# Two extra rows of the last weight matrix for half the partitions, and less work on VectorE, in a one-core decode layer

## The chip, the cores and the metric

The kernel runs on one core of a Trainium2 chip. The metric is the device time of one execution in microseconds, as the median of several runs. One further execution is profiled: its trace holds every instruction of the five engines (PE, the matrix engine; DVE, the vector engine; ACT, the scalar engine; POOL, GpSimd; SP, the queue engine that issues most transfers), every packet of the DMA engines, and every semaphore update. "The span" is the time from the first to the last recorded instruction of that execution.

## What is computed

One decode step of a transformer layer with four sequences and one token each: layer normalisation, attention of 32 query heads over the last 2048 rows of a cache with 4 key-value heads, a residual, a second layer normalisation, and a gated feed-forward block.

```python
D, Hq, Hkv, Sk, Dh, F = 1024, 32, 4, 8192, 128, 3584      # B = 4, Sq = 1, all bfloat16
W = 2048
q = (layernorm(x) @ wq).reshape(B, Sq, Hq, Dh).transpose(0, 2, 1, 3)
k = jnp.repeat(k_cache[:, :, Sk - W:, :], Hq // Hkv, axis=1)
v = jnp.repeat(v_cache[:, :, Sk - W:, :], Hq // Hkv, axis=1)
p = softmax(einsum("bhqd,bhkd->bhqk", q, k) * Dh ** -0.5)
h = x + einsum("bhqk,bhkd->bhqd", p, v).transpose(0, 2, 1, 3).reshape(B, Sq, Hq * Dh) @ wo
n = layernorm(h)
out = h + (silu(n @ w1) * (n @ w3)) @ w2
```

With four tokens there is little arithmetic for each weight. What has to be read is some 55.6 MB: 8 MB each of k, v, wq and wo (in units of 1,048,576 bytes, as below), and 7 MB each of w1, w3 and w2.

## The kernel before

**The ring of slots.** All large inputs pass through five slots of SBUF of 128 partitions x 32 KB (4 MB each). `ring` (line 107) lists what goes into them in order: k in two slots, half of wq, two slots for the transposed keys (no transfer), the other half of wq, v in two slots, wo in two, w1, w3 and w2 in two each. `fill` (line 119) issues the transfers on SP's queue, in the order of the list, as soon as all users of the slot five places earlier are done; `done` calls it after each user. Thus a transfer is issued when a slot comes free, and waits in the DMA queues behind those issued earlier.

**How w2 is cut.** w2 has 3584 rows of 1024 values (2 KB). Line 79 gives each of the 128 partitions 28 rows. They are loaded in pieces of 16, 8, 2 and 2 rows (`W2B`, line 108): the first piece fills one slot, the other three share the last one.

**Order of the work.** The schedule is written by hand: on every engine the instructions run in the order of the program.

- x is loaded by ACT's queue into `x_nat` (line 149), and the constants are made on DVE and GpSimd (lines 152 to 190).
- `layernorm_T` (line 192) is used twice. It works on transposed data; DVE makes nearly all steps.
- Lines 235 to 247: the keys are transposed by PE, block by block (8 matmuls each, 32 blocks), and copied out of PSUM by DVE and ACT in turn.
- Lines 250 to 282: the query projection, and the masked queries `Qm`.
- Lines 290 to 405: attention, one batch row after the other in a pipeline: `scores`, `row_max` (maximum, turned and shared out by two small matmuls), `softmax` (four exponentials on ACT, with their sums in `rs`), `transpose_p` on DVE, `output` (the sum's reciprocal, 16 matmuls over v, then `od` and `om` on DVE).
- Lines 406 to 444: the outputs are rearranged and multiplied by wo.
- Lines 450 to 482: the second layer normalisation, w1, the sigmoid (exponential, plus one, reciprocal, product), w3, the product `hg`, and its transposed form `hg_T`.
- Lines 485 to 504: the product with w2, piece by piece, the residual, and the store by two queues.

Each weight matmul handles a quarter of the output columns: four matmuls in four column groups of the array (`tile_position=(0, R * c)`) share one pass.

Of the kernel before, what the change touches and what calls it, by code (L numbers as in the profile page):

```python
# [10 lines left out]
P = 128  # L11
ACT = mybir.ActivationFunctionType
ALU = mybir.AluOpType
# [10 lines left out]
def kernel(  # L24
# [30 lines left out]
    FC = F // P  # L55
    NK = W // P
    C = 4
# [3 lines left out]
    FQ = F // C  # L61
    FH = FQ // 2
    assert B == C and Hkv == C and B * Hq == P and Dh == P and REP * Hkv == R
    assert D == KC * P and F == FC * P and W == NK * P and NQ == Hq * Dh
# [14 lines left out]
    w2_v = B_w2.rearrange("(p fc) n -> p fc n", fc=FC)  # L79
# [21 lines left out]
    wo_ = pair([("wo", g, [1, T * D], wo_v[:, g : g + 1, :]) for g in range(Hkv)])  # L101
# [6 lines left out]
    W2B = [16, 8, 2, 2]  # L108
# [5 lines left out]
    ring += [w2_[:1], w2_[1:]]  # L114
# [4 lines left out]
    def fill():  # L119

        while len(taken) < len(ring):
# [6 lines left out]
            for name, i, shape, src in parts:  # L128
# [3 lines left out]
                if src is not None:  # L132
                    nc.sync.dma_start(out=dst if name in ("k", "v") else view, in_=src)  # L133
# [6 lines left out]
    def done(name, i):  # L140
# [7 lines left out]
    nc.vector.memset(x_nat[:], 0.0)  # L148
    nc.scalar.dma_start(out=x_nat[::S, :], in_=x_flat.rearrange("b (c n) -> c b n", c=C))
    fill()  # L150

    ident = const.tile([P, P], BF16)
    make_identity(nc, ident[:])
    ones_f = const.tile([P, P], FP32)
    nc.vector.memset(ones_f[:], 1.0)
    eps_t = const.tile([P, 1], FP32)
    nc.vector.memset(eps_t[:], eps)

    t32 = const.tile([P, R], FP32)
    nc.vector.tensor_reduce(  # L160
        out=t32[:], in_=ident[:].rearrange("p (q h) -> p h q", q=C), axis=AX.X, op=ALU.add
    )
    ident_f = const.tile([P, P], FP32)
    nc.gpsimd.tensor_copy(out=ident_f[:], in_=ident[:])
    same = const.tile([P, C, R], FP32)
    for q in range(C):
        nc.gpsimd.tensor_copy(out=same[:, q], in_=t32[:])
# [4 lines left out]
    nc.vector.tensor_scalar(  # L172
# [3 lines left out]
    nc.vector.tensor_reduce(  # L176
        out=jmask[:, :, 0], in_=ident[:].rearrange("p (j h) -> p j h", j=JM), axis=AX.X, op=ALU.add
    )
    nscale = const.tile([P, Hkv], FP32)
    nc.vector.memset(nscale[:], -qscale)  # L180
# [3 lines left out]
    for l in range(2):  # L184
        nc.gpsimd.tensor_copy(
# [5 lines left out]

    def layernorm_T(h_T, tag):

        both = act.tile([P, 2, KC, B], FP32, tag=tag + "_both")
        nc.vector.tensor_copy(out=both[:, 0], in_=h_T[:, :, ::S])
        nc.vector.tensor_tensor(out=both[:, 1], in0=both[:, 0], in1=both[:, 0], op=ALU.mult)  # L196
        sums_ps = ps.tile([P, 2, KC, B], FP32, tag="kt3")
        nc.tensor.matmul(sums_ps[:], lhsT=ones_f[:], rhs=both[:], start=True, stop=True)  # L198
        sums = act.tile([P, 2, B], FP32, tag=tag + "_sums")
        nc.vector.tensor_reduce(  # L200
            out=sums[:], in_=sums_ps[:].rearrange("p t k b -> p t b k"), axis=AX.X, op=ALU.add
        )
        mean = act.tile([P, 2, B], FP32, tag=tag + "_mean")
        nc.vector.tensor_single_scalar(out=mean[:], in_=sums[:], scalar=1.0 / D, op=ALU.mult)
        rstd = act.tile([P, 1, B], FP32, tag=tag + "_rstd")
        nc.vector.tensor_tensor(out=rstd[:, 0], in0=mean[:, 0], in1=mean[:, 0], op=ALU.mult)
# [7 lines left out]
        hc = act.tile([P, KC, B], FP32, tag=tag + "_hc")  # L214
# [20 lines left out]
    for b in range(B):  # L235
        k = get("k", b)
        kT = get("kT", b)
        for jb in range(JR // JB):
# [3 lines left out]
            if n_step % 2 == 0:  # L242
                nc.vector.tensor_copy(out=kT[:, jb * JB : (jb + 1) * JB], in_=kt_ps[:])  # L243
            else:
                nc.scalar.copy(out=kT[:, jb * JB : (jb + 1) * JB], in_=kt_ps[:])  # L245
# [4 lines left out]
    q_ps = [ps.tile([P, REP // 2, Dh], FP32, tag=f"sc{hf}", name=f"q_ps{hf}") for hf in range(2)]  # L250
    HALF = REP // 2
    for i in range(KC // 4):
        w = get("wq", i)
        for kk in range(4):
            kc = 4 * i + kk
            for hf in range(2):
                for c in range(C):
                    o = (2 * c + hf) * HALF * Dh
                    nc.tensor.matmul(  # L259
                        q_ps[hf][R * c : R * c + R],  # L260
# [8 lines left out]
    nc.vector.tensor_copy(out=q_sb[:, :HALF], in_=q_ps[0][:])  # L269
    nc.scalar.copy(out=q_sb[:, HALF:], in_=q_ps[1][:])  # L270
# [7 lines left out]
    for b in range(B):  # L278
        nc.vector.tensor_copy(  # L279
            out=Qm[:, b].rearrange("p (g y) -> p g y", y=QW)[:, :, :REP],  # L280
# [254 lines left out]
```

## Time and profile before

| | |
|---|---|
| runs, median (3) | 139.9 us (139.68 to 140.05) |
| the profiled execution | 140.13 us |
| its span | 138.3 us |
| PE / DVE / ACT / POOL busy | 58% / 38% / 31% / 3% of the span |
| HBM read | 55.58 MB, 402 GB/s over the span |
| first data packet, last weight landing | 2.2 us, 134.26 us |

The costliest groups of instructions by busy time are ACT's exponentials (L334, 16 of them, 19.7 us), PE's matmuls over v (L369, 17.5 us), the key transposes (L241, 17.3 us), ACT's copies of the transposed keys (L245, 16 of 1.01 us) and DVE's (L243, 16 of 0.69 us). DVE's single longest instruction is the reciprocal of the sigmoid (L474, 5.75 us).

The profile page divides the span into 40 slices and gives for each engine the busy share in tenths; the DMA row is the mean over the core's 16 DMA engines. A line of a "windows" view has the stretch in microseconds, its length, the busy time (and number of instructions) of PE, PEld (weight loads), DVE, ACT and POOL, the granted clock of PE as a share of full speed, the DMA engines' mean share, and the rate. A line of the timeline has the start, the length, the engine, the line of the program, what was done, and in brackets the idle time before it and what ended it.

### The profile page before, as it was taken

The numbers are of one execution on the slowest core, as the hardware profiler recorded it, in microseconds if no ns is written. First come the engines' busy times: TensorE is split into PE (matmuls) and PEld (weight loads), VectorE is DVE, ScalarE is ACT, GpSimd is POOL, SyncE is SP. The second block draws the span as 40 slices with busy tenths as digits, with TensorE's granted clock in tenths as the row PEclk, the third lists the DMA queues.
The fourth block names the chain that finished last, engine by engine and source line by source line (L and its number), as shares of the span: only waits on it lengthen the run. The fifth ranks groups of instructions, "written<-read, shape, count | busy, mean of one in ns | idle before, by whom it ended". The sixth has DMA issues, their size and how long they took to land.

```text
span 138.3 us, 2012 instructions
## 1 busy us (share of the span) xinstructions
PE 80.2 (58%) x866; PEld 47.5 (34%) x868; DVE 52.9 (38%) x97; ACT 42.7 (31%) x57; POOL 4.2 (3%) x18
## 2 busy tenths in 40 slices
PE   0029898921903889328918998659539901703780
PEld 0029887820301322014304434537324400202550
DVE  3036676520000235177087197540330298350001
ACT  3005988850000325998807900000040200000000
POOL 7400000000000000000000000000000000000000
PEclk9999999998555799975797799965865896555555
DMA  4999999999989999999999999999999999999930
GB/s 152 399 423 431 431 436 455 455 441 398 445 384 426 441 417 417 450 407 431 450 400 431 433 469 431 394 448 448 419 398 448 456 411 430 445 407 398 406 148 2
DMA packets 3217, 55.72 MB, mean 403 GB/s; under 512 B 360, under 2 KB 392, under 8 KB 648
## 3 DMA queue, kind: packets, MB, share of 16 engines
q1 hardware_dynamic: 3178, 55.58, 94.4%
q8 instruction: 7, 0.11, 0.3%
q10 hardware_dynamic: 30, 0.01, 0.0%
q14 instruction: 2, 0.02, 0.0%
HBM read 55.58 MB, written 0.01 MB: 402 GB/s over the span
## 4 chain that ended last, share of the span: by engine, by line
DMA 49%; PE 27%; DVE 13%; ACT 4%; SPq 3%; issue 2%; DVEq 0%
DMA s_wq<-in_A_wq_dram 29%; DMA s_w<-in_B_w_dram 20%; PE o_ps L369 10%; PE y_ps L434 5%; ACT P L334 4%; PE sc_ps L294 3%; DVE PT L346 3%; SPq L133 3%; PE gu_ps L458 2%; PE q_ps L259 2%; DVE om L386 2%; DVE od L378 2%; PE on_ps L409 1%; PE tot_ps L355 1%; PE nm_ps L323 1%
## 5 line engine op out<-in xcount | busy, mean ns | idle before, releaser
L334 ACT ACTIVATE P<-sc_ps,bias 128x512 bf16<-128x512 f32 x16 | 19.7, 1417 | 9.6 <-DVE bias L331 9.6
L241 PE MATMUL kt_ps<-ident,s_k 128*128 128x128 bf16 x256 | 17.3, 228 | 1.3 <-ACT s_kT L245 1.0
L369 PE MATMUL o_ps<-s_v,PT 128*128 128x512 bf16 x62 | 17.5, 439 | 0.3 <-issue 0.2
L241 PEld LDWEIGHTS <-s_k 128*128 128x128 bf16 x256 | 16.3, 103 | 2.3 <-issue 1.7
L245 ACT COPY s_kT<-kt_ps 128x1024 bf16<-128x1024 bf16 x16 | 15.7, 1012 | 2.5 <-PE kt_ps L241 2.5
L458 PE MATMUL gu_ps<-s_w,n_T 128*32 128x448 bf16 x128 | 10.7, 513 | 8.8 <-DMA s_w<-in_B_w_dram 6.8
L259 PE MATMUL q_ps<-s_wq,n_T 128*32 128x512 bf16 x64 | 7.0, 615 | 11.8 <-DMA s_wq<-in_A_wq_dram 11.8
L243 DVE COPY s_kT<-kt_ps 128x1024 bf16<-128x1024 bf16 x16 | 11.1, 693 | 5.8 <-PE kt_ps L241 5.8
L491 PE MATMUL y_ps<-s_w,hg_T 128*32 128x256 bf16 x112 | 6.6, 418 | 8.0 <-DMA s_w<-in_B_w_dram 8.0
L369 PEld LDWEIGHTS <-PT 128*128 128x128 bf16 x64 | 7.2, 117 | 9.2 <-issue 4.4
L346 DVE STREAM_TRANSPOSE PT<-P 128x2048 bf16<-128x2048 bf16 x4 | 9.2, 2303 | 2.7 <-ACT P L334 2.7
L208 ACT ACTIVATE rstd<-rstd,eps_t 128x4 f32<-128x4 f32 x2 | 0.6, 297 | 29.5 <-DVE rstd L207 29.5
L458 PEld LDWEIGHTS <-n_T 128*32 128x32 bf16 x128 | 4.7, 131 | 14.1 <-issue 11.6
L294 PE MATMUL sc_ps<-s_kT,Qm 128*32 128x512 bf16 x64 | 8.5, 603 | 0.4 <-DVE Qm L279 0.4
L491 PEld LDWEIGHTS <-hg_T 128*32 128x32 bf16 x112 | 4.9, 142 | 10.0 <-issue 5.9
L259 PEld LDWEIGHTS <-n_T 128*32 128x32 bf16 x64 | 2.7, 137 | 15.6 <-issue 15.5
L269 DVE CAST q_sb<-q_ps 128x512 bf16<-128x512 f32 x1 | 0.7, 692 | 18.3 <-PE q_ps L259 18.3
L198 PE MATMUL sums_ps<-both,ones_f 128*128 128x64 f32 x4 | 1.1, 373 | 11.2 <-DVE both L196 11.2
L434 PE MATMUL y_ps<-s_wo,oP 128*32 128x256 bf16 x128 | 6.5, 397 | 1.7 <-DVE oP L422 1.7
L378 DVE SCALAR_TENSOR_TENSOR od<-o_ps,rinv,jmask 128x512 f32<-128x512 f32 x4 | 3.0, 751 | 8.4 <-PE o_ps L369 8.3
L270 ACT CAST q_sb<-q_ps 128x512 bf16<-128x512 f32 x1 | 0.6, 585 | 17.8 <-PE q_ps L259 17.8
L310 PE MATMUL mx_ps<-ident_f,rmax 128*1 128x128 f32 x8 | 1.7, 302 | 7.4 <-DVE rmax L308 7.4
(68 smaller groups left out, 64.7 us busy)
## 6 DMA issues: line engine op xcount, KB each, us to landing
s_w<-in_B_w_dram SPq DMA_DIRECT2D x4, 3584.0 KB, 21.2
s_k<-in_A_k_cache_dram SPq DMA_DIRECT2D x4, 2048.0 KB, 16.1
s_wq<-in_A_wq_dram SPq DMA_DIRECT2D x2, 4096.0 KB, 35.3
s_v<-in_A_v_cache_dram SPq DMA_DIRECT2D x4, 2048.0 KB, 25.1
s_wo<-in_A_wo_dram SPq DMA_DIRECT2D x4, 2048.0 KB, 25.5
s_w<-in_B_w_dram SPq DMA_DIRECT2D x1, 4096.0 KB, 28.0
s_w<-in_B_w_dram SPq DMA_DIRECT2D x1, 2048.0 KB, 25.7
s_w<-in_B_w_dram SPq DMA_DIRECT2D x2, 512.0 KB, 27.0
```

Of the source, the lines that this page charges most:

```text
L241: nc.tensor.transpose(out=kt_ps[:, jj], in_=k[:, jb * JB + jj, :], identity=ident[:])
L243: nc.vector.tensor_copy(out=kT[:, jb * JB : (jb + 1) * JB], in_=kt_ps[:])
L245: nc.scalar.copy(out=kT[:, jb * JB : (jb + 1) * JB], in_=kt_ps[:])
L259: nc.tensor.matmul(q_ps[hf][R * c : R * c + R], lhsT=xn_T[:, kc, :], rhs=w[:, kk, o : o + HALF * Dh], start=(kc == 0), stop=(kc == KC - 1) ...
L294: nc.tensor.matmul(sc_ps[b][R * q : R * q + R], lhsT=Qm[:, b, g * R : (g + 1) * R], rhs=v[:, g, q], start=(g == 0), stop=(g == Hkv - 1), t ...
L334: nc.scalar.activation(out=P4[:, :, :, g], in_=sc_ps[b][:].rearrange("p (j i) -> p j i", i=L5), func=ACT.Exp, bias=bias[:, g : g + 1], sca ...
L346: nc.vector.transpose(out=PT[:].rearrange("p j h -> p (j h)"), in_=stage.pop(("P4", b))[:].rearrange("p j i g -> p (j i g)"),)
L369: nc.tensor.matmul(o_ps[:], lhsT=PT[:, i * JM : (i + 1) * JM, :].rearrange("p j h -> p (j h)"), rhs=v[:, i * JM : (i + 1) * JM, :], start= ...
L378: nc.vector.scalar_tensor_tensor(out=od[:], in0=o_ps[:], scalar=rinv[:, 0:1], in1=jmask[:].to_broadcast([P, JM, Dh]), op0=ALU.mult, op1=AL ...
L434: nc.tensor.matmul(y_ps[R * c : R * c + R, :], lhsT=oP[:, g, t, :], rhs=w[:, 0, o : o + DQ], start=(g == 0 and t == 0), stop=(g == Hkv - 1 ...
L458: nc.tensor.matmul(out_ps[hf][R * c : R * c + R], lhsT=hn_T[:, kc, :], rhs=w[:, kk, o : o + FH], start=(kc == 0), stop=(kc == KC - 1), til ...
L491: nc.tensor.matmul(y2_ps[R * c : R * c + R, :], lhsT=hg_T[:, fc, :], rhs=w[:, ff, c * DQ : (c + 1) * DQ], start=(fc == 0), stop=(fc == FC ...
```

## The change

It has several parts.

1. **w2.** The 128-row grid loses a row: each partition holds 27 rows (pieces of 16, 7, 2 and 2), and the 128 rows that remain go to partitions 0 to 63, two rows each, as `w2x`. They are loaded by two transfers of 32 partitions, which are issued after the first piece of w2 and before the second. The source of each is ordered with an outer dimension of 8 (`e`), then 4 (`i`), then the two rows. The matching 128 columns of w1 and w3 are multiplied by separate matmuls of 64 columns in two of the four column groups; their values go through the sigmoid and the product in the last 64 columns of `eg` and `hg`, and are transposed by one more DVE instruction into `hx_T`. In the down projection 8 matmuls for `w2x` follow the first piece.
2. **wo** is loaded by two transfers of two groups instead of four of one.
3. **Softmax by pairs of rows.** Two batch rows share a PSUM tile of two banks. `row_max`, the new `bias_of` and the new `total` handle two rows at once; the masking term is added by a second small matmul, and the sums of the exponentials are added by PE. The loop over rows is replaced by a written order.
4. **Work given to ACT and GpSimd.** ACT copies 24 of the 32 key blocks instead of 16, the whole of `q_sb`, `on_sb` and `oP`, parts of the layer normalisation, the "plus one" of the sigmoid, and several constants. GpSimd clears `x_nat`, makes masks, and adds up the blocks of `od`. `Qm` is made by one copy instead of four.

DVE then has 66 instructions in its program instead of 118.

```diff
-    FC = F // P
+    FC = F // P - 1
+    FM = FC * P
+    XP = P // 2
+    XR = 2
...
-    FQ = F // C
+    FQ = FM // C
     FH = FQ // 2
+    FX = 32 * XR
...
-    w2_v = B_w2.rearrange("(p fc) n -> p fc n", fc=FC)
+    w2_v = B_w2[:FM].rearrange("(p fc) n -> p fc n", fc=FC)
+    w2x_v = B_w2[FM:].rearrange("(c i e y) n -> c e i (y n)", c=XP // R, i=4, e=8)
...
-    wo_ = pair([("wo", g, [1, T * D], wo_v[:, g : g + 1, :]) for g in range(Hkv)])
+    wo_ = [[("wo", i, [2, T * D], wo_v[:, 2 * i : 2 * i + 2, :])] for i in range(Hkv // 2)]
...
-    W2B = [16, 8, 2, 2]
+    W2B = [16, 7, 2, 2]
...
-    ring += [w2_[:1], w2_[1:]]
+    ring += [w2_[:1], [("w2x", 0, [XR, D], w2x_v)] + w2_[1:]]
...
-                if src is not None:
+                if name == "w2x":
+                    for c in range(XP // R):
+                        nc.sync.dma_start(out=dst[R * c : R * c + R], in_=src[c])
+                elif src is not None:
...
-    nc.vector.memset(x_nat[:], 0.0)
+    nc.gpsimd.memset(x_nat[:], 0.0)
...
-        nc.vector.tensor_copy(out=both[:, 0], in_=h_T[:, :, ::S])
-        nc.vector.tensor_tensor(out=both[:, 1], in0=both[:, 0], in1=both[:, 0], op=ALU.mult)
+        nc.scalar.copy(out=both[:, 0], in_=h_T[:, :, ::S])
+        nc.scalar.activation(out=both[:, 1], in_=h_T[:, :, ::S], func=ACT.Square)
...
-            if n_step % 2 == 0:
+            if n_step % 4 == 0:
                 nc.vector.tensor_copy(out=kT[:, jb * JB : (jb + 1) * JB], in_=kt_ps[:])
...
-    nc.vector.tensor_copy(out=q_sb[:, :HALF], in_=q_ps[0][:])
-    nc.scalar.copy(out=q_sb[:, HALF:], in_=q_ps[1][:])
+    nc.scalar.copy(out=q_sb[:], in_=q_ps[:].rearrange("p a r d -> p (a r) d"))
...
-    for b in range(B):
-        nc.vector.tensor_copy(
-            out=Qm[:, b].rearrange("p (g y) -> p g y", y=QW)[:, :, :REP],
-            in_=qT_ps[:, :, :, S * b].rearrange("p r g -> p g r"),
-        )
+    nc.vector.tensor_copy(
+        out=Qm[:].rearrange("p b (g y) -> p b g y", y=QW)[:, :, :, :REP],
+        in_=qT_ps[:, :, :, ::S].rearrange("p r g b -> p b g r"),
+    )
...
+    def bias_of(i):
+        nm_ps = ps.tile([P, 2, Hkv], FP32, tag="kt3")
+        nc.tensor.matmul(
+            nm_ps[:],
+            lhsT=stage.pop(("qmax", i))[:].rearrange("o q h -> o (q h)"),
+            rhs=nscale[:],
+            start=True,
+            stop=False,
+        )
+        nc.tensor.matmul(
+            nm_ps[:],
+            lhsT=ident_f[:],
+            rhs=negm[:].rearrange("p (o g) -> p o g", o=1).to_broadcast([P, 2, Hkv]),
+            start=False,
             stop=True,
         )
+        bias = act.tile([P, 2, Hkv], FP32, tag="bias", bufs=2)
+        nc.scalar.copy(out=bias[:], in_=nm_ps[:])
+        stage[("bias", i)] = bias
...
+    def total(i):
+        tot_ps = ps.tile([P, 2], FP32, tag="kt3")
+        for g in range(Hkv):
+            nc.tensor.matmul(
+                tot_ps[:],
+                lhsT=same[:].rearrange("p q h -> p (q h)"),
+                rhs=rs[:, 2 * i : 2 * i + 2, g],
+                start=(g == 0),
+                stop=(g == Hkv - 1),
+            )
+        nc.vector.reciprocal(out=rinv[:, 2 * i : 2 * i + 2], in_=tot_ps[:])
...
-        nc.vector.tensor_reduce(
-            out=om[:, b], in_=od[:].rearrange("p j d -> p d j"), axis=AX.X, op=ALU.add
-        )
+        o2 = act.tile([P, 2, Dh], FP32, tag="o2", bufs=1)
+        nc.gpsimd.tensor_tensor(out=o2[:], in0=od[:, :2], in1=od[:, 2:], op=ALU.add)
+        nc.gpsimd.tensor_tensor(out=om[:, b], in0=o2[:, 0], in1=o2[:, 1], op=ALU.add)
...
+    scores(0, (0, 1, 2, 3))
+    scores(1, (0, 1, 2, 3))
+    row_max(0)
+    scores(2, (0, 1))
+    bias_of(0)
+    softmax(0)
+    softmax(1)
+    scores(2, (2, 3))
+    scores(3, (0, 1, 2, 3))
+    row_max(1)
+    bias_of(1)
+    transpose_p(0)
+    transpose_p(1)
+    softmax(2)
+    softmax(3)
+    total(0)
+    output(0)
+    output(1)
+    transpose_p(2)
+    transpose_p(3)
+    total(1)
+    output(2)
+    output(3)
...
+                for c in range(XP // R):
+                    nc.tensor.matmul(
+                        out_ps[1][R * c : R * c + R],
+                        lhsT=hn_T[:, kc, :],
+                        rhs=w[:, kk, FM + c * FX : FM + (c + 1) * FX],
+                        start=(kc == 0),
+                        stop=(kc == KC - 1),
+                        tile_position=(0, R * c),
+                    )
...
-    nc.vector.tensor_scalar_add(out=eg[:], in0=eg[:], scalar1=1.0)
+    nc.scalar.activation(out=eg[:], in_=eg[:], func=ACT.Identity, bias=1.0)
...
+    hx_T = act.tile([XP, XR, R], BF16)
+    nc.vector.transpose(
+        out=hx_T[:].rearrange("p y r -> p (y r)"),
+        in_=hg[:XP, FQ:].rearrange("p (i e y) -> p y e i", i=4, e=8),
+    )
...
+        if i == 0:
+            for y in range(XR):
+                down(hx_T[:, y, :], get("w2x", 0)[:XP, y], False, False)
```

## The prediction

> **What bounds the kernel now.** I read the slices of the page first, then the DMA queues, the windows of the last microseconds, the timeline there, and last the waits.
>
> ```profile
> span 138.3 us, 2012 instructions
> ...
> PEclk9999999998555799975797799965865896555555
> DMA  4999999999989999999999999999999999999930
> ...
> DMA packets 3217, 55.72 MB, mean 403 GB/s; under 512 B 360, under 2 KB 392, under 8 KB 648
> ...
> q1 hardware_dynamic: 3178, 55.58, 94.4%
> q8 instruction: 7, 0.11, 0.3%
> ```
>
> The DMA row is at 9 from the second slice to the 38th, while no compute engine passes 58%. The chain of waits gives PE 27% and DVE 13%, but only because it walks back through a slot's release; in the DMA issues the last weights land 21 to 28 us after they are issued, so the queues held that much backlog and the release was no brake. This kernel ends when its bytes have landed, plus a tail. Now the windows of half a microsecond at the end (PE, PEld, DVE, ACT, POOL busy, clock, DMA share, GB/s):
>
> ```profile
> 131.50:132.00 0.50, 0.23 (x8) 0.20 (x11) 0.00 (x0) 0.00 (x0) 0.00 (x0) 0.50 0.84 336
> 132.00:132.50 0.50, 0.50 (x16) 0.44 (x12) 0.00 (x0) 0.00 (x0) 0.00 (x0) 0.50 0.55 221
> 132.50:133.00 0.50, 0.50 (x16) 0.42 (x12) 0.00 (x0) 0.00 (x0) 0.00 (x0) 0.50 0.48 197
> 133.00:133.50 0.50, 0.50 (x19) 0.44 (x12) 0.00 (x0) 0.00 (x0) 0.00 (x0) 0.50 0.47 180
> 133.50:134.00 0.50, 0.50 (x12) 0.27 (x5) 0.00 (x0) 0.00 (x0) 0.00 (x0) 0.50 0.11 41
> ```
>
> From 132.0 to 133.5 the share stands near one half: about half of the 16 DMA engines are done and the others are not. The trace's semaphore records say it by engine (each engine posts once for each transfer). The last transfer lands on seven engines at 132.24 to 132.46, then at 132.75, 133.06 and 133.52, and on six at 134.04 to 134.26. Followed back, the engines form two fixed groups of eight, 0.25 us apart from the first transfer on; call them early and late. The six of the late group fell a further 1.5 us back one by one, each just after one of the 16 KB packets of q8 (at 20.5, 29.7, 52.3, 87.4, 100.2, 112.9 us; the seventh, at 133.5, comes after the data). Those packets come every 197 to 279 executed PE instructions: PE's code. Two 8 KB instruction packets of q14 (69.9 and 77.7 us) cost one late and one early engine 0.7 to 0.8 us each.
>
> ```profile
> 126.88 3.61 PE L491 MATMUL y_ps<-s_w,hg_T 128*32 128x256 bf16 x64 [6.53 <-DMA s_w<-in_B_w_dram]
> ...
> 131.77 2.33 PE L491 MATMUL y_ps<-s_w,hg_T 128*32 128x256 bf16 x40 [1.28 <-DMA s_w<-in_B_w_dram]
> ...
> 134.30 0.62 PE L491 MATMUL y_ps<-s_w,hg_T 128*32 128x256 bf16 x8 [0.20 <-DMA s_w<-in_B_w_dram]
> ...
> 134.97 0.42 DVE L501 TENSOR_TENSOR res<-y_ps,h 128x256 bf16<-128x256 f32 x1 [12.06 <-PE y_ps L491]
> ```
>
> PE waits for weights before each piece of w2. After the last landing (134.26) come 8 matmuls, one addition and the store: 4.04 us to 138.3.
>
> **The change, part by part.**
>
> *w2.* One row of 2 KB leaves every partition (the second piece has 7 rows, packets of 14 KB instead of 16 KB), and partitions 0-63 get two, by two transfers of 32 packets of 4 KB. Packet records: 16 KB takes 0.611 us on its engine, 4 KB 0.160; 14 KB lies between by size: 0.611 - (2/12) x 0.451 = 0.536. An engine has 8 packets of the piece, so each of the 16 saves 8 x 0.075 = 0.60 us. Who pays depends on how many engines the transfers use. The source's outer dimension is 8. The load of x has an outer source dimension of 4 and each store one of 2, and the packets under 512 B count it out: 22 loads x 16 posts + 4 + 2 + 2 = 360, the number on the page. So I take 8 engines, each with 2 x 4 packets: 8 x 0.160 = +1.28. These eight end 1.28 - 0.60 = 0.68 us later, the other eight 0.60 us earlier. Which eight: x's packets stand between those of four engines of the early group, so I take the early group as the paying one. Bounds: with all 16 engines in it, nothing moves (0); with the late group paying, +0.68.
>
> The last landing then: late engines 134.26 - 0.60 = 133.66; early ones 132.46 + 0.68 = 133.14, the early one behind a q14 packet 133.06 + 0.68 = 133.74 (if that packet is ACT's, which stays; if DVE's, it should come too late to matter, since DVE has about half its instructions). Gain 0.52 to 0.60; I take **0.52**.
>
> The Trainium skill (DMA: Bandwidth & Descriptors, Rules for kernel authors) says that two transfers to disjoint partition halves aren't worth making, as both halves spray over all 16 engines; by that the sum is 0 and the time stays at 139.9. The same page (Why a DMA increments its semaphore by 16 and not by 1) lets the slowest dimension set the number of engines, lowest-numbered first, which agrees with the 360 posts above and gives the 0.52.
>
> *wo* by two transfers of 4 MB instead of four: same packets, 32 posts fewer, at 9 ns each 0.02 us an engine. Its later release (with g=3 of each pair) is 1.6 us later, against weights queued 21 us ahead: nothing.
>
> *PE.* Each up projection has 16 more matmuls of 64 columns. Eight matmuls of 448 take 0.75 us (0.093 each); 64 columns cost between 0.013 and 0.093, so 0.2 to 1.5 us; I take 0.4. The second one counts: it starts when w3 lands (117.17). hg_T was ready at 122.91 and waited until 126.88, 3.9 us of cover. In the down projection 8 matmuls come in and 4 go, 0.056 each (3.61/64): 130.49 + 0.45 = 130.94, before the next piece lands at 131.73 - 0.60 = 131.13. The 28 of that piece end near 132.8, the next 8 near 133.3, and the last landing still ends last. Without cover it would cost 0.45 us.
>
> *PE's code.* Softmax, totals and projections together add 40 matmul passes, each with a weight load: 80 instructions on 1748. The seventh refill was behind 1724 of them; now 104 remain behind it, so it falls at the end of the first w2 piece, about 130.5 us, with data still flowing. It costs an engine 1.5 us. On a late engine that none had hit: 132.75 - 0.60 + 1.5 = 133.65: free. Six refills had hit six different late engines, two remained; I take one of these. Bounds: 0, and 1.5 on an already late one.
>
> *K transposes.* ACT copies 24 of 32 blocks instead of 16 (L245, 1.01 us), DVE 8. Three copies on four blocks make 3.05 us; 8 such from 11.9 end at 36.3 instead of 29.6. Behind them waits v's first transfer, which must be queued before wq's last bytes run out (41.9): 5.6 us of cover, and 1 us for each us beyond. wq's matmuls need only be done by the second half at 43.86.
>
> *Attention.* q_sb by one ACT copy (about 1.0 instead of 0.70), Qm by one copy (0.45, as L422): scores start about 0.55 later, 49.4. Two rows of scores 3.6, a doubled maximum 1.2, then mx, qmax, nm and ACT's copies (0.3 each) about 2.1: the exponentials start near 56.3 instead of 53.3. But the old ones stood still twice (0.46 and 5.07 us, DVE bias L331), and now only once between pairs, behind ACT's own queue, about 1.1: 56.3 + 16 x 1.18 + 1.1 = 76.3 against 78.5. Outputs follow: 79.6 + 2 x 3.6 + od 0.75 and two GpSimd additions, which no row shows (between 0.4, two small copies, and 2.1, two of L386; I take 1.1, nearest L386): om at 89 as before (89.1), bounds -2 to +3. Its covers: the slot releases (w3's first half must be queued by 98 and was released at 87), then the 2.72 us for which hg waits for w3's matmuls (DVE L480), then the 3.9 us before w2. Nothing, up to there.
>
> *Layernorm, silu, setup.* DVE's work on ACT: some tenths of a us, in front of the same covers. The reciprocal over 928 columns costs 5.96 instead of 5.75, ahead of w3's landing. x's zeroing moves to GpSimd behind its constants: the load starts within 0.3 us of before, and the transposes wait for k anyway.
>
> **Sum.** Profiled execution: 140.13 us, span 138.3. Span 138.3 - 0.52 = 137.78, time 139.61; the median of the runs is 139.9, 0.23 below the profiled one: 139.38, say **139.4**.
>
> **Rivals.**
> 1. *Nothing moves.* The transfers use all 16 engines, or an engine that I don't see sets the end: 139.9. Against it the count of posts.
> 2. *The seventh refill takes the gain back* (the other side). Place: the engine that gets q8's packet near 130.5. On an engine already hit: 133.66 + 1.5 = 135.16, +0.90, 140.8; on an early one 133.14 + 1.5 = 134.64, +0.38, 140.3. It decides from the point where that engine would end later than 132.76 without it. For: the refill does move ahead of the data's end. Against: six of six went to fresh late engines.
> 3. *The late group pays:* 134.26 + 0.68 = 134.94, 140.6. Against it x's packets.
> 4. *Compute becomes the bound:* attention over 2.7 + 3.9 - 0.4 = 6.2 us later than before, each further us 1 us; with 8 late, 139.4 + 1.8 = 141.2. Against it ACT's shorter standstill.
>
> **How the numbers follow.** Forecast 0.62, rival 1 0.13, rival 2 0.12, rival 3 0.07, rival 4 0.06. The forecast's own range is 139.1 to 139.6. This kernel's runs tell 0.3% (0.42 us) from no change, and the forecast lies just beyond, so I give 0.09 of it to "same". Faster 0.53, same 0.09 + 0.13 + 0.02 = 0.24, slower 0.23. The range goes from 139.0 to 140.6, which leaves out the worst of rivals 2 and 4.
>
> **What would show it.** Right: in the last windows the DMA share falls from near 1 to 0 within half a us instead of standing at one half for 1.5; the last matmuls start near 133.7; posts under 512 B become 20 x 16 + 2 x 8 + 8 = 344. Wrong: 360 such packets (all 16 engines); an instruction packet near 130 followed by a lone late engine; a wait for hg_T instead of for DMA before the last matmuls; a DMA share under 9 near 42 us.

## The result and the profile after

The changed kernel takes **140.27 us** (median of 13 runs, 140.11 to 140.40) against 139.97 (139.57 to 140.11, 13 runs) of the kernel before: a ratio of 1.0024, 95% interval 1.0016 to 1.0032. It is slower by 0.3 us, less than the 0.3% that I had called the limit, but told apart by so many runs. The prediction was 139.4 and faster. The profiled execution takes 140.27 us, its span is 138.6 (before: 140.13 and 138.3).

The page of the changed kernel, the lines that answer to those shown of before:

```profile
span 138.6 us, 2090 instructions
...
PEclk9999999999955559995555995599869869985685
DMA  4999999999989999999999999999999999989920
...
DMA packets 3264, 55.72 MB, mean 402 GB/s; under 512 B 344, under 2 KB 376, under 8 KB 696
...
q1 hardware_dynamic: 3226, 55.58, 94.2%
q8 instruction: 7, 0.11, 0.3%
```

The kernel still ends with its bytes. 344 packets under 512 B is the forecast count to the packet: the extra rows use eight DMA engines. Seven refills of PE's code (q8) stand on both pages. That count hides the difference: in the trace the seventh starts at 131.99 us here and at 133.48 before, where only six engines were still at work and all of them behind the others already.

The last half-microseconds (columns as in the prediction: PE, PEld, DVE, ACT, POOL busy, clock, DMA share, GB/s):

```profile
131.50:132.00 0.50, 0.50 (x28) 0.50 (x20) 0.00 (x0) 0.00 (x0) 0.00 (x0) 1.00 1.02 393
132.00:132.50 0.50, 0.23 (x11) 0.03 (x1) 0.00 (x0) 0.00 (x0) 0.00 (x0) 1.00 0.75 303
132.50:133.00 0.50, 0.40 (x8) 0.20 (x8) 0.00 (x0) 0.00 (x0) 0.00 (x0) 1.00 0.29 115
133.00:133.50 0.50, 0.00 (x0) 0.00 (x0) 0.00 (x0) 0.00 (x0) 0.00 (x0) 1.00 0.13 25
133.50:134.00 0.50, 0.00 (x0) 0.00 (x0) 0.00 (x0) 0.00 (x0) 0.00 (x0) 0.85 0.02 8
```

The long shelf at one half, from 132.0 to 133.5 before, is gone: the share falls from 1.02 to 0.13 in 1.5 us (the forecast had named half a microsecond). What speaks against the forecast is the last row: 8 GB/s after 133.5. One engine out of 16 is still at work, alone. The timeline of the same stretch (start, duration, engine, what; in brackets the idle time before it and what ended it):

```profile
131.28 0.95 PE L545 MATMUL y_ps<-s_w2x,hg_T 128*32 128x256 bf16 x28 [0.62 <-DMA s_w2x<-in_B_w_dram]
...
132.59 0.40 PE L545 MATMUL y_ps<-s_w2x,hg_T 128*32 128x256 bf16 x8 [0.36 <-DMA s_w2x<-in_B_w_dram]
...
134.55 0.62 PE L545 MATMUL y_ps<-s_w2x,hg_T 128*32 128x256 bf16 x8 [1.56 <-DMA s_w2x<-in_B_w_dram]
...
135.21 0.42 DVE L564 TENSOR_TENSOR res<-y_ps,h 128x256 bf16<-128x256 f32 x1 [8.54 <-PE y_ps L545]
```

PE is idle for 1.56 us in front of its last 8 matmuls, and a DMA ends that wait. The semaphore records, one post by each engine for the last transfer, sort the sixteen:

```
                                 before                  after, forecast    after, measured
late engines, no refill          132.75 (133.52 w. q14)  132.15             131.61 131.98
early engines, no refill         132.24 to 132.46        133.14             132.84 to 133.08 (6)
late engines behind a refill     134.04 to 134.26 (6)    133.66             133.21 to 133.38 (6)
early one behind a q14 packet    133.06                  133.74             133.75
early one behind a refill        none                    134.64 (rival 2)   134.51
```

Fifteen engines are done by 133.75, against the forecast end of 133.74. The sixteenth ends at 134.51, 0.25 later than the last one before. That it is the refill's engine shows in the packet records: two 4 KB packets started at 133.00 and 133.43 take 441 and 429 ns instead of 160, and the second lasts past 133.75, when only one engine is left. One entry doesn't fit its row: 131.61 is 0.54 earlier than 132.15. By its time, that engine was probably one of the seven at 132.24 to 132.46 before (132.24 - 0.60 = 131.64), so the two groups that the prediction read off the times aren't quite the eight engines that carry the extra rows and the eight that don't. From here on, "early" means the eight that carry them.

### The profile page after: what moved, and what is told of

The parts are those of the page before. It is cut to its first block, busy times and chain, and to the rows that moved or that the text cites. A ratio compares the mean times of both kernels' runs of the same rounds, so it can differ in the third digit from the quotient of the medians.

```text
span 138.6 us, 2090 instructions
## 1 busy us (share of the span) xinstructions
PE 80.5 (58%) x908; PEld 51.6 (37%) x908; DVE 35.7 (26%) x46; ACT 56.9 (41%) x94; POOL 9.0 (7%) x29
## 4 chain that ended last, share of the span: by engine, by line
DMA 42%; PE 31%; ACT 11%; DVE 6%; SPq 4%; issue 1%; POOL 1%; POOLq 0%; DVEq 0%; ACTq 0%
DMA s_wq<-in_A_wq_dram 28%; DMA s_w2x<-in_B_w_dram 14%; PE o_ps L392 14%; ACT P L355 7%; PE y_ps L464 4%; SPq L143 3%; PE sc_psscA L305 3%; PE q_ps L271 3%; PE gate L489 2%; DVE PT L380 2%; PE tot_ps L369 1%; SPq L141 1%; DVE od L401 1%; PE on_ps L439 1%; ACT L220 1%
## 5 line engine op out<-in xcount | busy, mean ns | idle before, releaser
L257 ACT COPY s_kT<-kt_ps 128x1024 bf16<-128x1024 bf16 x24 | 22.3, 1091 | 1.2 <-PE kt_ps L253 1.2
L253 PE MATMUL kt_ps<-ident,s_k 128*128 128x128 bf16 x256 | 19.8, 242 | 4.2 <-ACT s_kT L257 3.4
L253 PEld LDWEIGHTS <-s_k 128*128 128x128 bf16 x256 | 18.4, 111 | 5.7 <-issue 5.7
L355 ACT ACTIVATE P<-sc_psscB,bias 128x512 bf16<-128x512 f32 x8 | 9.7, 1420 | 0.0
L355 ACT ACTIVATE P<-sc_psscA,bias 128x512 bf16<-128x512 f32 x8 | 9.7, 1410 | 0.0
L255 DVE COPY s_kT<-kt_ps 128x1024 bf16<-128x1024 bf16 x8 | 5.5, 694 | 14.1 <-PE kt_ps L253 14.1
L410 POOL TENSOR_TENSOR o<-od 128x256 f32<-128x256 f32 x4 | 2.9, 726 | 83.4 <-DVE od L401 83.4
L545 PE MATMUL y_ps<-s_w,hg_T 128*32 128x256 bf16 x64 | 3.6, 418 | 8.0 <-DMA s_w<-in_B_w_dram 8.0
L525 DVE RECIPROCAL eg<-eg 128x928 f32<-128x928 f32 x1 | 6.0, 5953 | 7.1 <-ACT eg L524 7.1
L489 PE MATMUL gate<-s_w,n_T 128*32 128x432 bf16 x64 | 5.0, 470 | 2.9 <-DVE n_T L230 2.9
```

Source lines behind the costliest of these rows:

```text
L253: nc.tensor.transpose(out=kt_ps[:, jj], in_=k[:, jb * JB + jj, :], identity=ident[:])
L355: nc.scalar.activation(out=P4[:, :, :, g], in_=sc_ps[b // 2][:, b % 2].rearrange("p (j i) -> p j i", i=L5), func=ACT.Exp, bias=bias[:, b % ...
L489: nc.tensor.matmul(out_ps[0][R * c : R * c + R, hf, :FH], lhsT=hn_T[:, kc, :], rhs=w[:, kk, o : o + FH], start=(kc == 0), stop=(kc == KC - 1),
L525: nc.vector.reciprocal(out=eg[:], in_=eg[:])
L545: nc.tensor.matmul(y2_ps[R * c : R * c + R, :], lhsT=lhsT, rhs=rows[:, c * DQ : (c + 1) * DQ], start=start, stop=stop, tile_position=(0, R ...
```

## The experiments

All times are medians; a ratio is to the kernel before on the same chip.

**Fewer PE instructions, nothing else.** e1_few takes 56 instructions off PE (the extra columns of w1 and w3 are then summed over the last of eight steps only), e2_pad puts as many back while PE waits for weights.

```
# e1_few, in up_projection
-                for c in range(XP // R):
+                for c in range(XP // R if kc == KC - 1 else 0):
...
-                        start=(kc == 0),
-                        stop=(kc == KC - 1),
+                        start=True,
+                        stop=True,
# e2_pad: e1_few, and while PE waits for wq
+        if i == 0:
+            pad_ps = ps.tile([P, JB, P], BF16, tag="kt0")
+            for jj in range(28):
+                nc.tensor.transpose(out=pad_ps[:, jj % JB], in_=ident[:], identity=ident[:])
```

> The changed kernel with 28 of its 32 small matmuls of 64 columns left out (the extra columns of gate and up are summed over the last of eight steps only, so their values are not those of the reference); PE runs 56 instructions less, everything else is as in the changed kernel. Theory T, the seventh refill of PE's code: with 56 instructions less in front of it the refill falls after the early engines' last data (later than 132.6 us), the last landing is the 133.7 us that the sum gave, and the time falls by 0.7 to 0.85 us, to 139.4 to 139.6. Rival U, compute: the matmuls left out cost PE some 2 us ahead of w2, but w2's first piece lands at 126.56 anyway, so 0 to 0.1 us less, 140.2. Rival V, the split itself made some engine late: no change, 140.27.

> The same with 28 transposes of the identity put in while PE waits for the second half of wq (near 38 us): the count of instructions ahead of the end is that of the changed kernel again, with none of the small matmuls. T: the refill falls before the data's end again, on an early engine, a last landing near 134.5, 140.2 to 140.4. U: as the run without the padding. V: 140.27.

e1_few: 140.21 (139.29 to 140.41, 12 runs), ratio 1.0008 [0.9990, 1.0026], and the runs fall into two groups: 139.29, 139.32 and 139.47, then nine from 139.97 to 140.41. Its profiled execution, of 139.29 us, lies 0.1 below the forecast of 139.4. Windows:

```profile
132.50:133.00 0.50, 0.45 (x12) 0.20 (x8) 0.00 (x0) 0.00 (x0) 0.00 (x0) 1.00 0.58 213
133.00:133.50 0.50, 0.00 (x0) 0.00 (x0) 0.00 (x0) 0.00 (x0) 0.00 (x0) 1.00 0.09 33
133.50:134.00 0.50, 0.18 (x8) 0.12 (x7) 0.00 (x0) 0.00 (x0) 0.00 (x0) 1.00 0.00 0
```

The transfers are over before 133.8; the last matmuls run at once, from 133.82. The seventh refill starts at 132.51 and stretches no packet. e2_pad: 140.32 (140.19 to 140.42, 6 runs), ratio 1.0030 [1.0019, 1.0041], an early engine at 134.43. So far this speaks for the seventh refill. But it explains neither the nine runs of e1_few near 140.2, nor e2_pad's profile: its seventh refill (131.55) stretches no packet either, and yet an early engine ends late.

**The rows on sixteen engines.** e3_sixteen asks rival 1's question, with the source in plain order.

```
-    w2x_v = B_w2[FM:].rearrange("(c i e y) n -> c e i (y n)", c=XP // R, i=4, e=8)
+    w2x_v = B_w2[FM:].rearrange("(c r y) n -> c r (y n)", c=XP // R, r=R)
...
-        in_=hg[:XP, FQ:].rearrange("p (i e y) -> p y e i", i=4, e=8),
+        in_=hg[:XP, FQ:].rearrange("p (r y) -> p y r", y=XR),
```

> The changed kernel with the rows of the two small transfers in plain order, so that the source's outer dimension is 32: T expects 16 posts for each (360 packets under 512 B instead of 344) and no shift between the two groups of engines: the six late engines land last at 134.2, the early one that the refill hits near 134.0, so the end is at 134.2, the time 0.2 to 0.3 less than the changed kernel's, 139.9 to 140.1. V (the split of the transfers is what costs): 139.9 or less. If the shift of 0.68 us was a gain by itself the time rises.

360 packets under 512 B, as forecast for sixteen engines, but 142.23 (141.81 to 142.52, 4 runs), ratio 1.0165 [1.0146, 1.0184]: the expectation is off by 2 us. Its windows while the extra rows arrive (the last column is GB/s):

```profile
125.00:125.50 0.50, 0.00 (x0) 0.00 (x0) 0.50 (x3) 0.00 (x0) 0.00 (x0) 0.50 1.52 303
125.50:126.00 0.50, 0.00 (x0) 0.00 (x0) 0.50 (x1) 0.00 (x0) 0.00 (x0) 0.50 0.39 74
126.00:126.50 0.50, 0.00 (x0) 0.00 (x0) 0.50 (x1) 0.00 (x0) 0.00 (x0) 0.50 0.47 123
126.50:127.00 0.50, 0.00 (x0) 0.10 (x1) 0.41 (x2) 0.00 (x0) 0.00 (x0) 0.50 0.68 229
127.00:127.50 0.50, 0.00 (x0) 0.00 (x0) 0.00 (x0) 0.00 (x0) 0.00 (x0) 0.50 1.40 336
```

For 2.5 us the core moves 74 to 336 GB/s, where its mean is near 400, and single 4 KB packets take up to 462 ns instead of 160. The next three windows move 213, 295 and 287 GB/s. At 403 GB/s the eight would have moved 1612 KB; they moved 930 KB, 1.7 us of transfer lost. By as much the first and the last landing of the last transfer are late (134.01 and 135.94; 132.24 and 134.26 in the kernel before). Why, no run here tells. The Trainium skill (DMA: Bandwidth & Descriptors, The descriptor swizzle) has each engine of a 128-partition transfer write its own group of partitions; the changed kernel's order of rows keeps that grouping, e3_sixteen sets two engines on each group, which would fit. The same page (Rules for kernel authors) advises against two transfers onto partition halves because both spray over all 16 engines: the 344 posts of the changed kernel show eight, and where there were sixteen it was worse still.

**The extra rows alone**, without the change's other parts (kernel before, with the rows of w2, their loads, projections, transposes and matmuls):

```
-    W2B = [16, 8, 2, 2]
+    W2B = [16, 7, 2, 2]
...
-    ring += [w2_[:1], w2_[1:]]
+    ring += [w2_[:1], [("w2x", 0, [XR, D], w2x_v)] + w2_[1:]]
```

> The kernel before with the extra rows of w2 alone (by two transfers with an outer dimension of 8); softmax, layer normalisation, copies and wo as before. PE has 73 instructions more than the kernel before, nearly as many as the changed kernel. T: the refill falls before the data's end and hits an early engine: 140.1 to 140.3, as the changed kernel. U: compute has its cover again, so the balance pays: 139.4.

140.44 (140.22 to 140.60, 6 runs), ratio 1.0038 [1.0025, 1.0051]. The loss is there without a changed softmax; two early engines end at 134.50 and 134.51.

**The rows without a seventh refill.** r6_whole_columns takes the extra rows as the 28th row of each partition, so the up projections stay as they were and PE's count stays below the seventh refill; r6_pad adds 40 transposes to bring it back; r7_change_short is the whole change in this form. (The rows then come in four transfers of 32 x 2 KB, still by eight engines; om and the strip of the output masks are bf16.)

```
# r6_whole_columns, against the kernel before
+    w2x_v = B_w2.rearrange("(y c i e fc) n -> c e i y fc n", y=XR, c=XP // R, i=4, e=8)[:, :, :, :, FM]
...
+                        for y in range(XR):
+                            nc.sync.dma_start(out=view[R * c : R * c + R, y], in_=src[c, :, :, y])
# r6_pad, against r6_whole_columns
+            for jj in range(40):
+                nc.tensor.transpose(out=pad_ps[:, jj % JB], in_=ident[:], identity=ident[:])
# r7_change_short, against the changed kernel: the rows as above, and the totals by one matmul
-        for g in range(Hkv):
-            nc.tensor.matmul(
...
+            rhs=rs[:, 2 * i : 2 * i + 2, :],
```

> The kernel before with the extra rows alone, written so that PE runs fewer instructions than the kernel before (6 less): w1 and w3 keep their 448-column matmuls, only the last of each partition's 28 rows moves, partitions 0-63 take their own and that of the partition 64 above them (four transfers of 32 packets of 2 KB, outer dimension 8), and the last matmuls of attention are in bfloat16. T, the refill: it comes after the data again, so nothing takes the balance's gain back: last landing 133.7 to 133.8, 139.4 to 139.5. V, the split costs by itself: 140.2 or more, as the two earlier kernels with it.

> The same with 40 transposes of the identity put in while PE waits for the second half of wq: 80 PE instructions more, 3 less than the changed kernel. T: the seventh refill is back before the data's end, on an early engine: 140.2 to 140.4, that is 0.8 more than without the padding. V: no difference between the two.

> The whole change (pairs of rows, ACT and GpSimd) with the extra rows taken as in the run before, the sums of a pair by one matmul, and the last matmuls of attention in bfloat16: PE runs 103 instructions less than in the changed kernel and 26 less than before. T: 139.3 to 139.5 in all executions, none near 140.3. U, attention's 6 us of lateness bind once the data ends earlier: 139.8 or more.

All three expectations of theory T missed. r6_whole_columns: 140.81 (140.15 to 141.32, 6 runs), ratio 1.0062 [1.0039, 1.0085]; r6_pad: 140.95 (140.79 to 141.07, 5 runs), 1.0072 [1.0056, 1.0088]; r7_change_short: 140.68 (139.78 to 140.95, 11 runs), 1.0048 [1.0033, 1.0063]. With six refills the loss is still there, and r7's profile has two early engines at 134.51 and 134.52 and only four late ones hit. So the theory that the first six refills always go to late engines falls. V, that the split costs by itself, and U fit these three times, but not the fast runs: 139.29 of e1_few has the split, and 139.78 of r7_change_short has the whole change. In its place came theory R of the next expectations: which engines are hit differs from execution to execution.

r6_whole_columns' own profile is of the fastest of its runs (140.15) and has no early engine behind a refill; the last landing is at 134.26 all the same. The posts of its four small transfers come from the eight engines that carry the rows: in the last of them six post at 126.27 to 126.59, the others at 127.07 and 127.42, and in the last transfer these two lags return as 133.91 and 134.26. They are probably the engines of the two q14 packets, which this kernel, with DVE's work as before, still has.

**Four of the kernels once more,** unchanged, one profiled execution each.

> The kernel before once more, one profile. Theory R: the refills of PE's code go to one DMA engine after the other, round all 16, and the engine that starts differs from execution to execution; so the engines that are 1.5 us late at the end are not always of the late group: hit engines near 133.9 to 134.0 if early, 134.1 to 134.3 if late; last landing 133.9 to 134.3. Theory T (the refills always hit the late group first): six engines at 134.0 to 134.3, as in the first profile.

> The changed kernel once more, one profile. R: the numbers of fresh late engines (131.6 to 132.0 in the last transfer), of late engines hit (133.2 to 133.4) and of early engines hit (134.5) differ from the first profile's 2, 6 and 1, with at least one early engine hit in all but about two of 16 starts; last landing 134.5. T: 2, 6 and 1 again.

> The kernel with 28 small matmuls less once more (the extra columns of gate and up again summed over the last step only), whose executions fell into two groups, 139.3 to 139.5 and 140.0 to 140.4, and whose profiled one was of the first. R: if the time is above 140, one or more early engines stand at 134.4 to 134.6 in the last transfer; if it is below 139.5, none does. T: at 139.3 none; no second group.

> The whole change with 103 PE instructions less once more. R: six refills, hit engines in another split than the first profile's two early and four late; time 140.6 to 140.9 with an early engine hit, 139.3 to 139.8 with none. T: the first profile's split again.

before_b 139.86, after_b 140.34, e1_few_b 140.19, r7_change_short_b 140.89. The very same program e1_few, 139.29 us in its first profile, now takes 140.19. Its windows, to be laid beside those above:

```profile
132.50:133.00 0.50, 0.45 (x19) 0.26 (x9) 0.00 (x0) 0.00 (x0) 0.00 (x0) 1.00 0.35 139
133.00:133.50 0.50, 0.27 (x8) 0.20 (x8) 0.00 (x0) 0.00 (x0) 0.00 (x0) 1.00 0.21 66
133.50:134.00 0.50, 0.13 (x7) 0.00 (x0) 0.00 (x0) 0.00 (x0) 0.00 (x0) 1.00 0.04 16
```

and the same last matmuls, by the timeline of e1_few and then of e1_few_b:

```profile
133.82 0.40 PE L545 MATMUL y_ps<-s_w2x,hg_T 128*32 128x256 bf16 x8 [0.87 <-DMA s_w2x<-in_B_w_dram]
```

```profile
134.48 0.62 PE L545 MATMUL y_ps<-s_w2x,hg_T 128*32 128x256 bf16 x8 [0.85 <-DMA s_w2x<-in_B_w_dram]
```

At 133.5 to 134.0 one engine still moves 16 GB/s where none did; it is an early one that lands at 134.44, with only five late ones hit. So R holds in what matters: the engines that are hit differ between executions of one program (R also said sixteen members; the part on the engines of the refills below finds eight). And before_b has an early hit too: one engine at 133.74 and five at 133.85 to 134.00 where the first profile had six at 134.04 to 134.26. There the end was no later for it.

**The rest of the change alone.** r8_no_extra_rows is the changed kernel with w2 as before; the main lines of the edit:

```
-    W2B = [16, 7, 2, 2]
+    W2B = [16, 8, 2, 2]
...
-    ring += [w2_[:1], [("w2x", 0, [XR, D], w2x_v)] + w2_[1:]]
+    ring += [w2_[:1], w2_[1:]]
```

> The changed kernel without part 1: w2 by four pieces of 16, 8, 2 and 2 rows for all partitions, no small matmuls; pairs of rows, wo by two transfers and the work on ACT and GpSimd as in the change. Theory R (the extra load meets refilled engines): without the extra load an early engine that a refill hits ends near 134.0 and a late one near 134.2, so the last landing is that of the kernel before, 139.8 to 140.0. Rival U (the other parts cost, attention is 6 us later): 140.2 to 140.4, as the change. A gain by the other parts: under 139.7.

140.05 (139.75 to 140.39, 12 runs) beside 139.99, ratio 1.0006 [0.9996, 1.0016]; last landing 134.17. Softmax by pairs, the work on ACT and GpSimd and the larger wo transfers change nothing that can be measured in the time. (The span is 0.2 us shorter, 138.0 against 138.2 in the median, and the time holds 2.0 us beyond the span instead of 1.8.)

**Which engines the refills take.** The records don't name the engine of a packet. But each of the first six refills stretches one large packet, and by how much (ns beyond the usual time of that size) gives a pattern:

```
refill            1    2    3    4    5    6     early engines at the end behind a refill
before           490  498  502  466  466  479                        0
before_b              494  506  466  459  479  547              1
after            493  497  503  459  459  479    1 (the seventh, 281)
e1_few           490  497  502  464  466  479    0
after_b               498  505  466  459  479  542              2 (one the seventh, 281)
e1_few_b              497  506  466  466  477  548              1
e2_pad      548  493  494  502  466  467                        1
r7_change_short  480  550  546  484  495  506                   2
```

Shifted against each other, the rows are one sequence: about 490, 497, 503, 466, 463, 479, 548, 548, and round again, begun at another place. The steps of about 548 are as many as the early engines hit, and where the seventh refill came in time, the next step of the sequence would be 548 too (the two 4 KB packets of the changed kernel are stretched by 281 + 269 = 550), and one more early engine is hit. The nine other profiles show the same sequence. Of all seventeen, nine begin at the second number of the sequence, five at the first, three elsewhere. That says: the refills go round **eight** engines, six late ones and two early ones, and the start differs by execution. It rests on a pattern of sizes, so three kernels put the rows elsewhere. They keep e1_few's projections and split the 128 rows otherwise, over as many engines as the outer dimension has: 4, 6 or 8. I number these from 0, and the posts show the counts. That a transfer over fewer than 16 engines takes the lowest-numbered ones is what the Trainium skill says (DMA: Bandwidth & Descriptors, Why a DMA increments its semaphore by 16 and not by 1); no record here names an engine, but the results below fit it.

```
# f1_six: 96 rows by engines 0-5, 32 rows by 0-7
+    w2a_v = B_w2[FM : FM + 96].rearrange("(c i e y) n -> c e i (y n)", c=2, i=4, e=6)
+    w2b_v = B_w2[FM + 96 :].rearrange("(i e) n -> e i n", i=4, e=8)
# f2_four: 64 rows by engines 0-3, 64 by 0-7
+    w2a_v = B_w2[FM : FM + 64].rearrange("(c i e y) n -> c e i (y n)", c=2, i=4, e=4)
+    w2b_v = B_w2[FM + 64 :].rearrange("(c i e) n -> c e i n", c=2, i=4, e=8)
# g1_half_row: 64 rows by engines 0-3, 64 as half rows on 128 partitions
+    w2a_v = B_w2[FM : FM + 64].rearrange("(c i e y) n -> c e i (y n)", c=2, i=4, e=4)
+    w2b_v = B_w2[FM + 64 :].rearrange("r (h n) -> (r h) n", h=2)
```

> As e1_few, but 96 of the 128 extra rows come by two transfers of 24 partitions (source's outer dimension 6: engines 0-5), and 32 by one of 32 partitions x 2 KB (engines 0-7). The matmuls use only the rows of partitions 0-23, so part of the sum over the extra rows is left out. Engines 0-5: 8 x 0.160 + 4 x 0.085 - 0.60 = +1.02, fresh 133.48; engines 6 and 7: 4 x 0.085 - 0.60 = -0.26, fresh 132.20, hit 133.70; late hit 133.66 as before. Theory A (a round of eight engines, its two early ones are 6 and 7): no engine after 133.75, or 134.08 where ACT's packet falls on one of 0-5; 139.5 to 139.8 in every execution, without the two groups of e1_few. Theory B (the round's early engines are among 0-5): most executions end on an early hit at 133.48 + 1.5 = 134.98, 140.6 to 140.8. Theory C (a round of all sixteen): early hits on six engines instead of eight, so 140.7 or 139.7 by the execution, with more of the lower group than e1_few's 3 of 12.

> As f1_six, but 64 rows by two transfers of 16 partitions (outer dimension 4: engines 0-3) and 64 by two of 32 partitions x 2 KB (engines 0-7). Matmuls use the rows of partitions 0-15 only. Engines 0-3: 1.28 + 0.68 - 0.60 = +1.36, fresh 133.82; engines 4-7: +0.08, fresh 132.54, hit 134.04; late hit 133.66. Theory A: the end at 134.04 where the execution's round hits 6 or 7, else 133.82, or 134.42 if ACT's packet falls on one of 0-3: 139.5 to 140.1. Theory B with the early engines among 4 and 5: the same as A here, while f1_six gives 140.7; with them among 0-3: 133.82 + 1.5 = 135.32, 141.0 to 141.1. Theory C: between 139.6 and 141.1 by the execution, half of the early hits at 135.32.

> As f2_four, but the 64 rows that went by engines 0-7 go back to all sixteen: as half rows of 1 KB on 128 partitions, one transfer. Matmuls use the extra rows of partitions 0-15 only, so part of the sum over the extra rows is left out. If a 1 KB packet takes about 0.05 us (2 KB took 0.085, 4 KB 0.160): late engines -0.60 + 0.40 = -0.20, hit 134.06; engines 4-7 the same, hit 133.76; engines 0-3 another 1.28: fresh 132.46 + 1.08 = 133.54, with ACT's packet 134.14. Theory of the round of eight with its early engines off 0-3: the end at 134.1 in every execution, 139.8, spread no wider than 0.4. If the refills also reach engines 0-3: 133.54 + 1.5 = 135.04 in most executions, 140.8.

f1_six: 140.76 (139.91 to 141.05, 10 runs), ratio 1.0042 [1.0022, 1.0061], three runs at 139.91 to 140.10 and seven from 140.64 up: at least one early engine of the round carries more here, so it is among 0-5. f2_four: 140.44 (140.25 to 140.72, 10 runs), 1.0027 [1.0018, 1.0037]: 0.3 above the range that theory A gave, which stays open, but with no group at 141.0, so the round's early engines are not among 0-3. Its profile has one step of 539 and, as computed for an engine of 4-7, a landing at 133.98 (134.04); its end, 134.34, is the engine with ACT's packet, which is among 0-3 (134.42). The posts of its small transfers say the same without the run times: those on four engines come at 125.53 to 125.57 and, behind ACT's packet, 126.24; those of the first one on eight engines come at 125.28 to 125.89, at 126.57 (ACT's packet) and at 126.85. The last is the early hit, some 1.5 us behind its neighbours, and it isn't one of the four. Together with f1_six, at least one early engine of the round is 4 or 5. g1_half_row keeps engines 4 to 15 light: 139.97 (139.81 to 140.07, 10 runs), 1.0000 [0.9990, 1.0009], last landing 133.97 (134.1 expected), and the spread of 0.26 us has no second group. With the rows off the round the loss is gone.

No kernel here beats the one before in all its executions; g1_half_row, the best, can't be told from it. In its profile the late engines behind refills end at up to 133.80 and the engine with ACT's packet at 133.97, so by my estimate (133.97 - 133.80) another split of the rows has a tenth or two of a microsecond left to gain. None was tried.

## Why the prediction was wrong

**The step that failed** is the one on PE's code: "Six refills had hit six different late engines, two remained; I take one of these." The refill itself was forecast, with its price (1.5 us; measured, a gap of about 1.0 and packets longer by 0.5). It was put 1.5 us too early (130.5, measured 131.99). The outcome of an early hit was forecast too (134.64, measured 134.51; 140.3, measured 140.27). The choice of engine was wrong. I read six hits of one execution as a rule about the late group. The runs show a round, by all signs one of eight with two early members. Seven refills in a round of eight leave out one engine, so at least one early engine is hit in any execution, which agrees with 13 runs of which none came below 140.11. Rival 2 was right about the outcome and should have had the larger chance. About the cause it was right in part: in the profile above it is the seventh refill that hits an early engine, but in after_b the sixth has already hit one, and in e2_pad the seventh does no harm and the time is 140.32 all the same.

**Why a hit on an early engine was harmless before** follows from the same numbers. It used to end at 132.46 + 1.5 = 133.96 by reckoning, below the late ones at 134.26; before_b and r8_no_extra_rows show it, with an early hit at 133.74 and 133.83 and ends at 134.00 and 134.17. The end was that of the late group whichever engines the round began with. The change moved some 0.6 us onto the early group (0.68 by the sum; its latest engine without a refill or a q14 packet went from 132.46 to 133.08) and so took the early hits from harmless to last. This also means that the forecast gain of 0.52 is real (e1_few, 139.29), but only where neither early engine is hit while data flow and no q14 packet takes the hit's place as in r6_whole_columns: by their times, 3 of 12 runs of e1_few and 1 of 11 of r7_change_short.

**Right:** the kernel is bound by its bytes; eight engines, 344 posts; the early group pays (132.84 to 133.08 for 133.14, while late engines behind refills ended 0.3 us earlier than the forecast 133.66); DVE's own instruction packet gone from the run; wo and the other edits free, which r8_no_extra_rows shows as a whole.

**Right by luck:** the early engine behind a q14 packet, 133.75 for 133.74. The sum took it from the engine that ended at 133.06, on the condition that its packet was ACT's. It was DVE's: that engine falls back between the transfers whose first landings are at 76.2 and 81.1 us, so behind the packet at 77.7. The packet at 69.9 is ACT's: it comes behind 49 ACT instructions, as does the one of the changed kernel at 36.73. ACT's packet had cost its engine 0.96 us before (the one at 133.52) and costs an early one about 0.7 now; that this is about what DVE's packet had cost is chance.

**A sign that couldn't speak:** a DMA share under 9 near 42 us. The DMA row is not at 9 throughout, as I read it: its 12th slice (38 to 41.5 us) is at 8 before and after.

**Wrong in size, without cost:** attention. I had it end as before, with bounds of -2 and +3. The timeline:

```profile
71.00 9.43 PE L392 MATMUL o_ps<-s_v,PT 128*128 128x512 bf16 x32
...
81.21 4.49 DVE L380 STREAM_TRANSPOSE PT<-P 128x2048 bf16<-128x2048 bf16 x2
...
83.57 9.98 PE L392 MATMUL o_ps<-s_v,PT 128*128 128x512 bf16 x32 [2.35 <-DVE PT L380]
...
104.60 0.42 DVE L475 TENSOR_TENSOR h<-y_ps,x_nat 128x256 f32<-128x256 f32 x1 [6.29 <-PE y_ps L464]
...
126.44 0.23 DVE L535 STREAM_TRANSPOSE hx_T<-hg 64x64 bf16<-64x64 bf16 x1
```

Two pairs of outputs take 9.4 and 10.0 us, where I had put 2 x 3.6 = 7.2 for a pair from the profile before. That 3.6 was taken at a granted clock of 1.00 (79.1 to 82.7 us); over the two pairs the clock is 0.75 and 0.70. The clock row above stands at 5 in six of the slices from 62 to 90 us (the 19th to the 26th), where that of the kernel before has one 5. The second pair also waits 2.35 us for transposes that stand on DVE behind the first pair's od. h1 comes at 104.60 instead of 98.84, 5.8 us later and beyond the bound. It cost nothing: of the covers that I had counted (2.72 and 3.9 us), hg_T used the last up, ready at 126.5 instead of 122.9, but the first w2 matmul still starts at 126.60, and after its 72 matmuls PE waits 0.62 us for the next piece.

## What to carry to other kernels

When a kernel ends with its bytes, balance the DMA engines for the engine that is disturbed last, not for the average: a delay of 1.5 us that falls on other engines in other executions can't be balanced against in one of them. What looks like slack on the faster engines may be the room for that delay. A pattern seen six times in one profile is one observation, since its six parts share one start; a second profile of the same kernel costs little and would have shown it.

## What the hardware showed that I had not expected

- A refill of PE's code costs its DMA engine 1.5 us and moves round eight engines, begun at different ones in different executions; the same program ended 0.9 us apart by it (139.29 and 140.19). The Trainium skill (Runtime: NRT & Kernel Launch, Instruction fetch mechanics) calls crossing a block of code mostly hidden. For PE that agrees: in the profile before, 0.2 us of its matmuls' waits are put down to nothing that the profile shows. For a DMA engine at the end of a transfer it does not: 1.5 us. The pattern of eight is inferred from stretched packets and from three placements, not read off a record; that the engines hit differ between executions is in the landings themselves.
- A transfer onto 32 partitions by sixteen engines instead of eight: up to 462 ns for a 4 KB packet that otherwise takes 160, and the whole core at 74 to 336 GB/s for 2.5 us.
- Left open: what sets the start of the round; and why r6_whole_columns and r7_change_short, with packets of 2 KB in four transfers, lie 0.5 and 0.4 us above the changed kernel's median. For r7_change_short most of it lies outside of the span: the spans are alike (138.6), and the time holds 2.0 us beyond it instead of 1.7.
